# Where the norm work of a fused attention and mixer kernel stands between the exponentials

## The chip, the cores and the metric

The kernel runs on one core of a Trainium2 chip. The metric is the device time of one execution in microseconds (us), the median of five runs. The engines are named as the profile names them: PE (TensorE; PEld is its weight load), DVE (VectorE), ACT (ScalarE), POOL (GpSimd) and SP (SyncE, which here only issues transfers).

## The reference

The input is q, k and v of 8 batches, 12 heads, 448 positions and 64 features, in float32. For each head, rows of q and k are divided by their norm, and attention with temperature tau = 0.1 is taken over them. The heads are then joined to x of 448 x 768 per batch, and a mixer follows.

```
q_n = q / (norm(q) + 1e-6);  k_n = k / (norm(k) + 1e-6)
attn = softmax(q_n @ k_n.T / 0.1);  x = attn @ v         # heads joined to [8, 448, 768]
h = relu(x.T @ w_tok1) @ w_tok2;    u = x + h.T          # w_tok1 448x256, w_tok2 256x448
out = u + relu(u @ w_ch1) @ w_ch2                        # w_ch1 768x1536, w_ch2 1536x768
```

## The kernel before, in words

**Pairs and slots.** The work is cut into 48 pairs of heads, six for a batch. The main loop has one slot for each pair, `i`. In slot i the scores of pair i are made, the product with v of pair i-1 is taken, and the two token matmuls follow for an earlier pair. After the six pairs of a batch its channel mixer (`m_ch1`, `m_ch2`) stands in a queue, from which `feed` takes pieces and puts them between the attention steps of later slots. Everything is in one written order (`tc.manual_schedule`): each engine carries out its own instructions in the order of the program text, and semaphores between engines keep the data right.

**One slot on PE and ACT.** `score(i, c)` for c = 0, 1, 2 makes two matmuls into a tile `psS`, of which there are two buffers, and one exp on ACT (line 298, `pt<-psS`). `score_x(i)` makes one more matmul and exp (line 305, `psX`). Because there are two `psS` buffers, the second matmul pair of slot i+1, `score(i+1, 1)`, can start only when the exp of `score(i, 2)` has been taken. ACT also takes the relu of each `m_ch1` piece (line 387, `gt<-psG`). `next_qk(i+1)` transposes the scaled q and k of the next pair on PE into `pst` (line 239 for the 384 main positions, lines 243 and 244 for the 64 others) and DVE copies them out (line 257). `pv` writes `psO`; DVE takes a reciprocal and multiplies (lines 323 and 324). `m_tok1` writes `psR`, which DVE turns to `r` (line 341); `m_tok2` multiplies `r` (line 357, `psU`).

**The norm work.** A pair p is prepared some slots ahead in four steps:

- `norm_begin(p)`: the squares of q and of k (line 174 on ACT, line 176 on DVE or POOL) into a tile `sq` of two buffers. A pair with p % 3 = 0 also squares the 64 rest positions of its half of a batch, three pairs together, into the single tile `sqx`.
- `norm_sums(p)`: DVE sums them over the features (line 189; line 193 for `sqx`).
- `rnorms(n, c0, c1)`: for half n (three pairs, 45 columns) ACT makes ln, exp, ln, exp (lines 197 to 200) on columns c0 to c1, which gives the inverse norms. Columns 0 to 21 hold the rest positions and the first pair, 21 to 45 the two other pairs. This is called a round below, and a round over columns 0 to 21 or 21 to 45 half a round.
- `norm_scale(p)`: POOL multiplies k and q by them into `kq` (line 207; lines 213 and 218 for the rest positions of a half). For pairs below 15 PE transposes `kq`, later ones go by transposing transfers.

Tables give the slot of each step: `early_sq` for the squares, `sum_at` one slot later, `rn_at` for the rounds, `sc_at` for the scaling (two slots before the pair's own slot up to pair 14). In slots 1 to 5 and from 7 on the loop body was, in this order: scores 0 and 1, sums, rounds, squares and scaling (in this or the other order), casts of v, and then the rest of the slot with `score(i, 2)`. Slot 6 (`FIRST`) has a body of its own.

The lines that matter in the old text:

```
early_sq = {3: 0, 4: 1, 5: 1, 6: 3, 7: 4, 8: 5, 9: 6, 10: 7, 11: 7, 12: 8, 13: 9, 14: 9, 15: 10, 16: 11, 17: 11}
sum_at = at({p: s + 1 for p, s in sq_slot.items()})
for c0, c1 in ((0, 21), (21, 45)) if n < 6 else ((0, 45),):
    s = 1 + sq_slot[3 * n + (0 if c1 == 21 else 2)]
```

Of the kernel before, what the change touches and what calls it, by code (L numbers as in the profile page):

```python
# [22 lines left out]
def kernel(  # L23
# [12 lines left out]
    nc = tc.nc  # L36
# [16 lines left out]
    NPAIR = H // 2  # L53
# [16 lines left out]
    ps = ctx.enter_context(tc.tile_pool(name="ps", bufs=4, space=bass.MemoryType.PSUM))  # L70
# [107 lines left out]
    def squares(p, eq, ek):  # L178
        sq[p] = nrm.tile([P, 2, 2 * NC, E], FP32, name=f"sq_{p}", tag="sq")
        for a, (eng, src) in enumerate(((eq, mh(qm, p)), (ek, mh(km, p)))):  # L180
            square(eng, sq[p][:, a], src.rearrange("p g c e -> p (g c) e"))
# [13 lines left out]
    def rnorms(n, c0=0, c1=45):  # L195
        ssq, rn = ssqs[n % 3][:, c0:c1], rns[n % 3][:, c0:c1]
        nc.scalar.activation(out=rn, in_=ssq, func=AF.Ln, bias=tiny[:])
        nc.scalar.activation(out=rn, in_=rn, func=AF.Exp, scale=0.5)
        nc.scalar.activation(out=rn, in_=rn, func=AF.Ln, bias=eps[:])
        nc.scalar.activation(out=rn, in_=rn, func=AF.Exp, scale=-1.0)  # L200
# [90 lines left out]
    def score(p, c, fill=0):  # L291
        qk, pt = qks[p], pts[p % 2]
        psS = ps2.tile([P, 2, 512], FP32, name=f"psS_{p}_{c}", tag="s")
        busy(psS[:, 0, :], fill)
        for g in range(2):
            r = slice(E * g, E * g + E)
            nc.tensor.matmul(psS[:, g, 0:S], qk[r, P * c:P * (c + 1)], qk[r, 512:512 + S], start=True, stop=True)  # L297
        nc.scalar.activation(out=pt[:, 2 * S * c:2 * S * (c + 1)].rearrange("p (g s) -> p g s", g=2),  # L298
                             in_=psS[:, :, 0:S], func=AF.Exp, scale=inv_tau)

    def score_x(p):
        qk, pt = qks[p], pts[p % 2]
        psX = ps.tile([P, 512], FP32, name=f"psX_{p}", tag="b")
        nc.tensor.matmul(psX[:, 0:S], qk[:, P * NC:P * (NC + 1)], qk[:, 512:512 + S], start=True, stop=True)  # L304
        nc.scalar.activation(out=pt[:, PX:PX + S], in_=psX[:, 0:S], func=AF.Exp, scale=inv_tau)  # L305
# [28 lines left out]
    def m_tok1(p):  # L334
        psR = ps.tile([P, TT, P], FP32, name=f"psR_{p}", tag="b")
        for tt in range(TT):
            for m in range(NC + 1):
                nc.tensor.matmul(psR[:, tt, :], w1t[:, m, tt * P:(tt + 1) * P], xs[p][:, m, :],  # L338
                                 start=(m == 0), stop=(m == NC))
        rs[p] = att.tile([P, TT, P], FP16, name=f"r_{p}", tag="r")  # L340
        nc.vector.tensor_scalar_max(out=rs[p][:], in0=psR[:], scalar1=0.0)  # L341
# [83 lines left out]
    def feed(budget, least=0.0):  # L425
        fed[0] += budget
        done = 0.0
        while queue and (fed[0] > queue[0][0] / 2 or done < least):
            t, fn = queue.pop(0)
            fn()  # L430
            fed[0] -= t
            done += t

    def at(slots):
        got = {}
        for p, s in slots.items():
            got.setdefault(s, []).append(p)
        return got


    FIRST = NPAIR
    early_sq = {3: 0, 4: 1, 5: 1, 6: 3, 7: 4, 8: 5, 9: 6, 10: 7, 11: 7, 12: 8, 13: 9, 14: 9, 15: 10, 16: 11, 17: 11}
    sq_slot = {p: early_sq.get(p, p - 6) for p in range(3, NP_ALL)}
    sq_at = at(sq_slot)
    sum_at = at({p: s + 1 for p, s in sq_slot.items()})

    rn_at = {}
    for n in range(1, NHALF):
        for c0, c1 in ((0, 21), (21, 45)) if n < 6 else ((0, 45),):
            s = 1 + sq_slot[3 * n + (0 if c1 == 21 else 2)]  # L450
            rn_at.setdefault(s, []).append((n, c0, c1))
    sc_at = at({p: {7: 6}.get(p, p - 2 if p < DMA_FROM else p - 3) for p in range(3, NP_ALL)})
# [14 lines left out]
    def norm_begin(p, eq, ek):  # L467
        squares(p, eq, ek)
        if p % HP == 0:
            squares_x(p // HP, eq, ek)  # L470

    def norm_sums(p):
        sums(p)
        if p % HP == 0:
            sums_x(p // HP)
# [6 lines left out]
    with tc.manual_schedule():  # L482
# [77 lines left out]
        for i in range(NP_ALL + 2):  # L560
            for n in qk_at.get(i, ()):
                load_q(n)
                load_k(n)
            for b in x_at.get(i, ()):
                load_xq(b)
                load_xk(b)
            for n in v_at.get(i, ()):
                load_v(n)
            for b in xv_at.get(i, ()):
                load_xv(b)  # L570
            if DMA_FROM <= i + 2 < NP_ALL:
                dma_tpose(i + 2)
            if i - 2 in X_DMA:
                x_tpose(i - 2)
            for p in ut_at.get(i, ()):
                u_tpose(p)

            left = next((t + 1 - i for t in sorted(tok2_at) if t >= i + (i == FIRST) and
                         any(p % NPAIR == NPAIR - 1 for p in tok2_at[t])), 6)
            if FIRST <= i < 2 * NPAIR:  # L580
                quota = max(len(queue) - 6, 0) * ns(S, DT) / (2 * NPAIR - i)
            else:
                quota = max(sum(t for t, _ in queue) - 2000.0, 0.0) / left
            def next_qk(p):
                if p < min(DMA_FROM, NP_ALL):
                    qk_copy(p, tpose(p))

            def tok2(p):
                m_tok2(p)
                if p % NPAIR == NPAIR - 1:  # L590
                    queue.extend(ch_units(p // NPAIR))

            def norm_rn():
                for n, c0, c1 in rn_at.get(i, ()):
                    rnorms(n, c0, c1)

            if i == FIRST:
                m_tok1(i - 2)
                pv(i - 1, 0)
                pv(i - 1, 1)  # L600
                tok2(i - 2)
                m_tok1(i - 1)
                next_qk(i)
                tok2(i - 1)
                for p in sum_at[i]:
                    norm_sums(p)
                feed(0.0, 1000.0)
                score(i, 0)
                norm_rn()
                score(i, 1)  # L610
                feed(0.0, 1000.0)
            elif 0 < i < NP_ALL:
                score(i, 0, 2 if i < 4 else 0)
                score(i, 1)
            if i != FIRST:
                for p in sum_at.get(i, ()):
                    norm_sums(p)
                norm_rn()

            if i >= FIRST:  # L620
                for p in sc_at.get(i, ()):
                    norm_scale(p, nc.gpsimd)
            for p in sq_at.get(i, ()):
                norm_begin(p, nc.scalar if p < 18 else nc.gpsimd, nc.scalar if p == 3 else nc.vector if 9 <= p < 12 else nc.gpsimd)
            if i < FIRST:
                for p in sc_at.get(i, ()):
                    norm_scale(p, nc.gpsimd)
            for n in cast_at.get(i, ()):
                cast_v(n)
            if i in (2, 5):  # L630
                weights_ch1(i // 4)
            if i in (7, 8):
                weights_ch2(i - 7)

            if i < FIRST:
                if i:
                    pv(i - 1, 0)
                if i:
                    score(i, 2)
                    score_x(i)  # L640
                if i + 1 < FIRST:
                    next_qk(i + 1)
                for p in tok_at.get(i, ()):
                    m_tok1(p)
                if i:
                    pv(i - 1, 1)
                for p in tok2_at.get(i, ()):
                    tok2(p)
            elif i == FIRST:
                score(i, 2)  # L650
                score_x(i)
                feed(0.0, 1000.0)
                next_qk(i + 1)
                feed(0.0, 1000.0)
            else:
                feed(quota * 0.25)
                next_qk(i + 1)
                if i <= NP_ALL:
                    pv(i - 1, 0)
                for p in tok_at.get(i, ()):  # L660
                    m_tok1(p)
                feed(quota * 0.25, 400.0)
                if i < NP_ALL:
                    score(i, 2)
                    score_x(i)
                for p in tok2_at.get(i, ()):
                    tok2(p)
                feed(quota * 0.25)
                if i <= NP_ALL:
                    pv(i - 1, 1)  # L670
                feed(quota * 0.25)
            if i == 2:
                place_w2()
# [38 lines left out]
```

## Time and profile before

| what | value |
|---|---|
| median of 5 runs | 408.36 us (408.28 to 410.18) |
| the profiled execution | 409.4 us, its span 407.3 us |
| granted PE clock, mean | 0.985 |
| PE busy | 390.9 us, 96% of the span |
| ACT, POOL, DVE busy | 228.5 us, 208.2 us, 203.2 us |
| slots on PE | slot 6 from about 40, slot 7 from 51.03, 8 from 54.95, 9 from 62.12, 10 from 67.45, 11 from 72.85, 12 from 81.44 us |

In the profile's timeline a row gives the start in us, the length, the engine, the line, the output and input tiles, the shape and a count (`x2` is two instructions merged in one row). Square brackets at its end give the idle time of the engine ahead of the row, and which instruction ended it. The start of a slot is read as the start of its first two `psS` matmuls. PE matmuls overlap in the records, so a wait is better measured between the starts of rows than by the bracket.

### The profile page before, as it was taken

Reading aid. Unit: us, or ns where it says so; the run is one execution under the profiler, and the core shown is the slowest. Engines: PE = TensorE matmul, PEld = TensorE weight load, DVE = VectorE, ACT = ScalarE, POOL = GpSimd, SP = SyncE. Lnnn points to the kernel's source line nnn. Section 1 sums busy time; section 2 is a strip of 40 time slices with the busy share of each in tenths; the row PEclk is TensorE's granted clock in tenths of the full one; section 3 lists DMA queues with packets and bytes.
Section 4 is the critical chain, followed back from the end, with each engine's and each line's share of the span. In section 5 each row is a group of like instructions: output and inputs, shape, how many; then the busy total and the mean of one; then the engine's idle time right before and its main releaser. Section 6 shows DMA issues by size and latency. Waiting matters only on the chain.

```text
span 407.3 us, 9113 instructions
## 1 busy us (share of the span) xinstructions
PE 390.9 (96%) x3646; PEld 226.4 (56%) x3646; DVE 203.2 (50%) x461; ACT 228.5 (56%) x415; POOL 208.2 (51%) x308
## 2 busy tenths in 40 slices
PE   7699989999999999999999999999999999999995
PEld 2366446565555564565555565565555565565562
DVE  5688668565445555436453655446444343232021
ACT  5898599863566547574566445664756435611400
POOL 4877369992093858567592928567673500000000
PEclk9689999999999999999999999999999999999999
DMA  8999999979893798979896698969882643013012
GB/s 218 260 229 258 254 228 207 247 146 226 161 256 76 228 168 214 183 154 203 174 269 101 194 167 202 221 141 236 183 144 50 138 99 66 15 54 103 2 77 77
DMA packets 137194, 67.51 MB, mean 166 GB/s; under 512 B 93184, under 2 KB 133568, under 8 KB 137152
## 3 DMA queue, kind: packets, MB, share of 16 engines
q1 hardware_dynamic: 132976, 61.36, 70.0%
q0 software_dynamic: 3632, 5.18, 7.1%
q8 instruction: 28, 0.46, 0.5%
q10 hardware_dynamic: 544, 0.39, 0.3%
q14 instruction: 14, 0.11, 0.1%
HBM read 43.38 MB, written 11.01 MB: 134 GB/s over the span
## 4 chain that ended last, share of the span: by engine, by line
PE 75%; POOL 7%; ACT 6%; issue 4%; DVE 4%; DMA 3%; SPq 1%; ACTq 0%; POOLq 0%; DVEq 0%
PE psF L399 24%; PE psG L385 23%; PE psO L318 7%; PE psS L297 7%; PE psR L338 4%; PE psU L357 4%; ACT pt L298 3%; PE psX L304 3%; DMA xq<-in_q_dram 2%; POOL kq L207 2%; PE psO L320 2%; POOL sq L176 2%; POOL kq L218 1%; DMA km<-in_k_dram 1%; POOL sqx L176 1%
## 5 line engine op out<-in xcount | busy, mean ns | idle before, releaser
L298 ACT ACTIVATE pt<-psS 128x896 f16<-128x896 f32 x141 | 123.9, 915 | 72.1 <-PE psS L297 71.9
L385 PE MATMUL psG<-ut,wc1t 128*128 128x448 f16 x576 | 122.5, 353 | 0.0
L399 PE MATMUL psF<-wc2t,gt 128*128 128x384 f16 x672 | 117.1, 326 | 0.6 <-ACT pt L305 0.6
L387 ACT ACTIVATE gt<-psG 128x448 f16<-128x448 f32 x96 | 52.1, 544 | 78.5 <-PE psG L385 78.3
L207 POOL TENSOR_TENSOR kq<-km,rn 128x384 f16<-128x384 f32 x47 | 39.0, 829 | 105.1 <-ACT rn L200 100.9
L399 PEld LDWEIGHTS <-gt 128*128 128x128 f16 x672 | 63.4, 98 | 42.6 <-issue 4.7
L385 PEld LDWEIGHTS <-wc1t 128*128 128x128 f16 x576 | 52.5, 98 | 46.0 <-issue 5.4
L402 DVE TENSOR_TENSOR ost<-psF,ur 128x384 f32<-128x384 f32 x56 | 31.2, 557 | 82.0 <-PE psF L399 79.1
L318 PEld LDWEIGHTS <-pt 128*128 128x128 f16 x1152 | 52.6, 98 | 16.6 <-issue 5.7
L318 PE MATMUL psO<-vt,pt 128*128 128x65 f16 x1152 | 58.2, 195 | 0.0
L189 DVE TENSOR_REDUCE ssq<-sq 128x12 f32<-128x768 f32 (+1 forms) x49 | 45.2, 931 | 17.2 <-POOL sq L176 14.4
L297 PE MATMUL psS<-qk 64*128 64x448 f16 x282 | 44.3, 361 | 3.1 <-ACT pt L298 3.1
L324 DVE TENSOR_TENSOR x<-psO,rec 128x256 f16<-128x256 f32 x96 | 40.8, 425 | 3.3
L320 PE MATMUL psO<-vx,pt 128*128 128x130 f16 x192 | 42.1, 219 | 0.0
L207 POOL TENSOR_TENSOR kq<-qm,rn 128x384 f16<-128x384 f32 x47 | 38.8, 826 | 0.0
L323 DVE RECIPROCAL rec<-psO 128x4 f32<-128x4 f32 x96 | 17.1, 178 | 42.4 <-PE psO L320 42.1
L176 POOL TENSOR_TENSOR sq<-km 128x384 f32<-128x384 f32 x43 | 35.3, 822 | 2.9 <-DMA km<-in_k_dram 2.7
L367 DVE TENSOR_TENSOR ut<-psU,xT 128x448 f16<-128x448 f32 (+2 forms) x39 | 17.6, 477 | 25.3 <-PE psU L357 18.5
L338 PE MATMUL psR<-x,w1t 128*128 128x128 f16 x384 | 29.4, 219 | 0.1
L297 PEld LDWEIGHTS <-qk 64*128 64x128 f16 x282 | 10.8, 94 | 33.1 <-issue 28.8
L357 PE MATMUL psU<-w2t,r 128*128 128x448 f16 x96 | 25.9, 353 | 1.7 <-DVE r L341 0.7
L305 ACT ACTIVATE pt<-psX 128x448 f16<-128x448 f32 x48 | 26.1, 544 | 0.0
(75 smaller groups left out, 340.4 us busy)
## 6 DMA issues: line engine op xcount, KB each, us to landing
vm<-in_v_dram SPq DMA_DIRECT2D x16, 576.0 KB, 6.7
out_dram<-ost SPq DMA_DIRECT2D x24, 384.0 KB, 2.9
qm<-in_q_dram SPq DMA_DIRECT2D x15, 576.0 KB, 4.9
km<-in_k_dram SPq DMA_DIRECT2D x15, 576.0 KB, 6.8
wc1t<-in_moe_w_ch_dram POOLq DMA_DIRECT2D x2, 1152.0 KB, 13.5
wc2t<-in_moe_w_ch_dram POOLq DMA_DIRECT2D x2, 1152.0 KB, 12.7
out_dram<-ost SPq DMA_DIRECT2D x8, 192.0 KB, 2.8
xq<-in_q_dram SPq DMA_DIRECT2D x7, 192.0 KB, 8.9
```

The lines of the kernel that those rows point to most:

```text
L176: eng.tensor_tensor(out=out, in0=src, in1=src, op=ALU.mult)
L189: nc.vector.tensor_reduce(out=ssqs[p // HP % 3][:, lo + 6 * a0:lo + 6 * a1], in_=sq[p][:, a0:a1].rearrange("p a g e -> p (a g) e"), axis=A ...
L207: eng.tensor_tensor(out=kqs[n % 2][:, j, a, 0:NC, :].rearrange("p c (g e) -> p g c e", g=2), in0=src, in1=_bcast_free(rn, E), op=ALU.mult)
L297: nc.tensor.matmul(psS[:, g, 0:S], qk[r, P * c:P * (c + 1)], qk[r, 512:512 + S], start=True, stop=True)
L298: nc.scalar.activation(out=pt[:, 2 * S * c:2 * S * (c + 1)].rearrange("p (g s) -> p g s", g=2), in_=psS[:, :, 0:S], func=AF.Exp, scale=inv ...
L318: nc.tensor.matmul(psO[:, mm, E1 * g:E1 * (g + 1)], pt[:, at:at + P], vt[:, 2 * j + g, c, 0:E1], start=(g == 0 and c == 0), stop=False)
L320: nc.tensor.matmul(psO[:, mm, :], pt[:, PX + lo:PX + lo + P], vx[:, j, 0:2 * E1], start=False, stop=True)
L338: nc.tensor.matmul(psR[:, tt, :], w1t[:, m, tt * P:(tt + 1) * P], xs[p][:, m, :], start=(m == 0), stop=(m == NC))
L357: nc.tensor.matmul(psU[:], rs[p][:, tt, :], w2t[:, tt, lo:lo + S], start=(tt == 0), stop=by_dma and tt == TT - 1)
L385: nc.tensor.matmul(psG[:], wc1t[:, dt, ct * P:(ct + 1) * P], ut[:, dt, sp], start=(dt == 0), stop=(dt == DT - 1))
L387: nc.scalar.activation(out=gt[:, ct, sp], in_=psG[:], func=AF.Relu)
L399: nc.tensor.matmul(psF[:], gt[:, ct, lo:lo + P], wc2t[:, ct, dh * DH:(dh + 1) * DH], start=(ct == 0), stop=(ct == CT - 1))
```

## The change

The norm work of pairs 9 to 17 is written at other places, and the rounds of halves 4 and 5 are joined.

- Pair 9: its squares stand at the head of slot 6 (they were in the middle of it), q on ACT and k on POOL (k was on DVE). Its sums follow the second score of slot 6, and its half round, `rnorms(3, 0, 21)`, follows in slot 6 after the third `feed`. It was in slot 7.
- Pair 10: squares at the end of slot 6 (were in slot 7), sums behind them.
- Pairs 11 to 17: squares in the slot that they were in (pair 11 in slot 7, 12 in 8, 13 and 14 in 9, 15 in 10, 16 and 17 in 11), but behind the last exp of the slot instead of behind the rounds; sums at the end of that slot instead of in the next one.
- The half round `rnorms(3, 21, 45)` stays in slot 8. Halves 4 and 5 get one round of 45 columns, in slots 10 and 12, for two half rounds each, in slots 9 and 10 and in 11 and 12.
- The squares of k of pairs 12 and 15, and of their rest positions, go from POOL to DVE. Those of pairs 10 and 11 stay on DVE.

The order of instructions on PE and on SP is the same in both kernels. ACT has eight instructions less, DVE two more and POOL two less. Waits on semaphores differ where the order behind them does.

```diff
-    early_sq = {... 8: 5, 9: 6, 10: 7, 11: 7, 12: 8, ...}
+    early_sq = {... 8: 5, 9: 5, 10: 6, 11: 7, 12: 8, ...}
...
-    sum_at = at({p: s + 1 for p, s in sq_slot.items()})
+    sum_at = at({p: s + 1 for p, s in sq_slot.items() if p < 8 or p >= 18})
...
-        for c0, c1 in ((0, 21), (21, 45)) if n < 6 else ((0, 45),):
+        for c0, c1 in ((0, 21), (21, 45)) if n < 4 else ((0, 45),):
...
+            def next_sq(ps):
+                for p in ps:
+                    norm_begin(p, nc.scalar if p < 18 else nc.gpsimd, nc.scalar if p == 3 else nc.vector if p in (10, 11, 12, 15) else nc.gpsimd)
+
             if i == FIRST:
+                next_sq([9])
                 m_tok1(i - 2)
...
-                for p in sum_at[i]:
-                    norm_sums(p)
+                norm_sums(8)
                 feed(0.0, 1000.0)
                 score(i, 0)
-                norm_rn()
+                rnorms(2, 21, 45)
                 score(i, 1)
+                norm_sums(9)
                 feed(0.0, 1000.0)
...
-            for p in sq_at.get(i, ()):
-                norm_begin(p, nc.scalar if p < 18 else nc.gpsimd, nc.scalar if p == 3 else nc.vector if 9 <= p < 12 else nc.gpsimd)
+            if i < FIRST or i >= 2 * NPAIR:
+                next_sq([p for p in sq_at.get(i, ()) if p != 9])
...
                 score(i, 2)
                 score_x(i)
                 feed(0.0, 1000.0)
+                rnorms(3, 0, 21)
                 next_qk(i + 1)
+                next_sq(sq_at[i])
+                norm_sums(10)
                 feed(0.0, 1000.0)
...
                     score(i, 2)
                     score_x(i)
+                if i < 2 * NPAIR:
+                    next_sq(sq_at[i])
                 for p in tok2_at.get(i, ()):
                     tok2(p)
                 feed(quota * 0.25)
                 if i <= NP_ALL:
                     pv(i - 1, 1)
+                if i < 2 * NPAIR:
+                    for p in sq_at[i]:
+                        norm_sums(p)
                 feed(quota * 0.25)
```

## The prediction

> **What bounds the kernel now.** I read the page first: its busy times name PE.
>
> ```profile
> PE 390.9 (96%) x3646; PEld 226.4 (56%) x3646; DVE 203.2 (50%) x461; ACT 228.5 (56%) x415; POOL 208.2 (51%) x308
> ```
>
> PE has no slack over the span, so a change of norm work can only take away time in which PE stands. The change lies between 40 and 82 us; there I read the PE timeline, and for each bracket in it the timeline of the engine that it names.
>
> ```profile
> 51.03 0.55 PE L297 MATMUL psS<-qk 64*128 64x448 f16 x4
> ...
> 54.95 0.36 PE L297 MATMUL psS<-qk 64*128 64x448 f16 x2
> 56.46 0.37 PE L297 MATMUL psS<-qk 64*128 64x448 f16 x2 [1.14 <-ACT pt L298]
> 56.76 0.51 PE L239 MATMUL pst<-id,kq 128*128 128x128 f16 x6
> 57.99 0.23 PE L243 MATMUL pst<-id,kq 128*128 128x128 f16 x1 [0.72 <-POOL kq L218]
> ...
> 66.28 0.55 PE L357 MATMUL psU<-w2t,r 128*128 128x448 f16 x2 [0.21 <-DVE r L341]
> ...
> 68.09 0.37 PE L297 MATMUL psS<-qk 64*128 64x448 f16 x2 [0.28 <-ACT pt L298]
> ```
>
> Slot 7 shows a free start: four psS matmuls in 0.55, so the second two begin 0.19 behind the first. From starts: slot 8's second pair came at 56.46 instead of 55.14, a loss of 1.32; its line 243 at 57.99 instead of 57.10 (0.34 behind line 239, as elsewhere), 0.89; slot 9's psU at 66.28 instead of 65.91, 0.37; slot 10's second pair at 68.09 instead of 67.64, 0.45; slot 11's four took 0.79, 0.24. Together 3.27 us. Cross-check: slots 8, 9 and 10 last 7.17, 5.33 and 5.40, and less these losses 4.96, 4.96 and 4.95, for equal work. From 82 to 407 us the waits list gives PE three waits, together 1.7 us.
>
> ```profile
> 53.18 0.32 ACT L197 ACTIVATE rn<-ssq,tiny 128x21 f32<-128x21 f32 x1
> ...
> 54.26 0.92 ACT L174 ACTIVATE sq<-qm 128x384 f32<-128x384 f32 x2
> 55.08 0.52 ACT L387 ACTIVATE gt<-psG 128x448 f16<-128x448 f32 x1
> 55.51 0.91 ACT L298 ACTIVATE pt<-psS 128x896 f16<-128x896 f32 x1
> ```
>
> This is slot 7 on ACT. A half round takes 1.08 (53.18 to 54.26), two squares 0.82, and only then comes the exp that frees the psS buffer for 56.46. With three exps at 0.81, the exp of psX 0.43 and one relu 0.43, ACT needs 5.19 us in such a slot, more than PE's 4.95. The half round of half 3 ends at 54.35, so POOL's scaling of pair 9 runs 54.48 to 57.93: the second wait.
>
> **The change, part by part.** I lay the new order out with the same step lengths. Start to start on ACT: exp 0.81, psX 0.43, relu 0.43, square 0.41, round 1.08. On DVE: sums 0.86, rest sums 0.66, copy of pst 0.58, reciprocal and multiply 0.55. On POOL: 0.79, four steps of a pair with rest positions 3.45.
>
> Slot 6: pair 9's squares cost nothing. ACT stands from 40.0 to 45.15 and POOL from 40.4 to 47.66; q and k of half 3, issued at 26.87 and 27.46, landed 6.2 and 7.4 us later. Without that cover the squares would hold ACT for 0.8. Sums of pair 9 end on DVE at 46.9. ACT then runs exp 48.69, psX, relu, half round 50.35 to 51.43, square of pair 10, relu, and slot 7's exps from 52.27, 0.7 later than before; slot 7's third scores (53.87) need the first of them, done at 53.2.
>
> Slot 7: the relu ends at 54.38 and `score(7, 2)`'s exp at 55.20, because no half round stands before it. Slot 8's second pair starts at 55.27: 1.32 becomes 0.13, a gain of 1.19. POOL scales pair 9 from 51.65 to 55.10, and line 243 would come at 55.91: 0.89 goes. Running gain 2.08; slot 9 would start at 60.05.
>
> Slot 8: exps from 56.04, half round 57.66 to 58.75, relu, third exp 59.2, psX, squares 60.43 to 61.25. POOL scales pair 10 from 58.97 to 60.6, and PE reaches its q part at 60.71. DVE squares k of pair 12 from 58.57, and then waits for ACT: sums from 61.0. Its chain (sums, rest sums, copy, reciprocal, multiply, r) puts r at 63.7 and psU at 64.1, where PE would be at 63.8. So the wait at psU stays at about 0.3; only its cause is new.
>
> Slots 9 to 11: slot 9 has no round, so the third exp ends in time and 0.45 goes; slot 11 loses its half round and 0.24 goes. Pairs 13 and 14 add two sums at the end of slot 9, ahead of the copy of pair 11; DVE follows psU's late start, so slot 10's r comes about 0.2 after PE wants it. That is given back.
>
> Slot 10: the joined round waits for pair 14's sums (about 67.7 to 68.0). Behind it in ACT's queue stand a relu, the third exp and psX, which PE wants only 2.6 later; behind its result stands POOL's scaling of pair 12, 3.45 long, ending at 72.5, where PE wants the last part at about 72.5. Before, this scaling had 4 us of slack (done at 71.04, used at 75.05). So the cover is gone.
>
> Without contention the sum is 2.08 + 0.45 + 0.24 less about 0.3 given back: 2.5 us.
>
> **DVE against POOL.** The squares of k of pairs 10, 11, 12 and 15 are now DVE instructions with two SBUF inputs beside a busy POOL. In the old stretch DVE's three such squares ran at 0.55 while POOL stood still. One place in the trace has both busy:
>
> ```profile
> 10.78 0.82 POOL L176 TENSOR_TENSOR sq<-km 128x384 f32<-128x384 f32 x1
> 11.56 0.66 POOL L213 TENSOR_TENSOR kq<-xq,rn 64x256 f16<-64x256 f32 x1
> ```
>
> ```profile
> 10.86 0.89 DVE L213 TENSOR_TENSOR kq<-xq,rn 64x128 f16<-64x128 f32 x1 [0.67 <-ACT rn L200]
> ```
>
> DVE's 0.89 compares with about 0.29 by the line through its free rows (0.55 at 384 elements, 0.35 at 192): it stood until POOL's instruction ended at 11.60. POOL's next lost some 0.05 (0.66 against 0.61 by its own line), so a 384 element square may cost POOL about 0.3. The bounds for a square are 0 and a whole POOL instruction, 0.82. I take the row. Pairs 10 and 11 have room. Pair 12: POOL's q part ends at 60.85 instead of 60.6, so PE waits 0.2. Pair 15: POOL's scaling of pair 12 ends some 0.45 later, and PE waits 0.5 to 0.6. Together about 0.7, which leaves 1.8 us.
>
> [...]
>
> From slot 12 on: pair 15's scaling waits for the joined round of slot 12 and ends near 86 us instead of 82.4, but SP issues its transposing transfer only at 92.96 (about 91 now), so 5 us of cover remain. POOL then stood from 94.3 to 111.57, which takes up the delay. The weight transfers on POOL's queue (59.77 and 63.55) are issued some 3 us earlier. SP's order is the same; its q load for half 6 waits for pair 11's scaling, which comes earlier. Everything later follows PE, so the gain stays.
>
> The profiled execution took 409.4 with a span of 407.3, 1.0 above the median; I subtract the difference from the median: 408.36 - 1.8 = 406.6. Its span should fall to about 405.5.
>
> **The rivals.** *No contention worth counting*: 2.5 us, and 3.1 if the r chain also keeps up: 405.2 to 405.9. For it: the squares may fall between POOL's instructions. Against it: the row at 10.86.
>
> [...]
>
> *The joined round holds the queue* (slower). If pair 14's sums come late, ACT stands at line 197 with exps behind it, and POOL's scaling of pair 12 and PE's transposes follow one for one. Sums at 70 instead of 68 take the gain away; at 71.3 or later it is slower by over 0.3%. What could do it is POOL, which must issue a transfer (0.88), scale pair 11 (1.6) and square two k (1.6) between 60.6 and 66. By these rows it is done at 64.7, which speaks against it. Price at 3.5 us lateness: 408.36 - 1.8 + 3.5 = about 410.
>
> **How the numbers follow.** Forecast 0.5, no contention 0.2, the stall moves 0.2, the queue 0.1. About 0.3%, 1.23 us, is what a measurement of this kernel can tell from no change; faster means below 407.13. The forecast's own range, from the bounds of contention, is 406.0 to 407.2. Faster gets all of the second case and nearly all of the first, with a little of the third: 0.72. Same 0.18, slower 0.1. The range 405.2 to 407.8 takes in the second case and most of the third.
>
> **What would show it.** Right: slot 8's two psS pairs within 0.35 of each other; line 243 of slot 8 without a bracket; slots 9 to 11 free of ACT's brackets; POOL's scaling of pair 9 ending near 55; a wait of about 0.5 on POOL at slot 11's line 243, and DVE's squares of pairs 12 and 15 above 0.55. Wrong: an exp bracket still above 0.5 in slots 8 to 11, ACT idle in front of line 197 for over 1 us in slot 10, or new PE waits behind 82 us.

## The result and the profile after

The changed kernel takes 406.86 us (27 runs, 405.75 to 409.39) where the kernel before, run on the same chip, takes 408.80 us: a ratio of 0.9954, 95% interval 0.9943 to 0.9965. A second set of runs gave 0.9954 again (0.9920 to 0.9987). The profiled execution has a span of 404.8 us, against 407.3.

The page's first lines, of the changed kernel:

```profile
PE 389.4 (96%) x3646; PEld 225.7 (56%) x3646; DVE 205.2 (51%) x463; ACT 226.5 (56%) x407; POOL 208.9 (52%) x306
```

PE bounds it as before. Its timeline, at the places that the prediction named:

```profile
53.96 0.79 PE L297 MATMUL psS<-qk 64*128 64x448 f16 x4
54.68 0.51 PE L239 MATMUL pst<-id,kq 128*128 128x128 f16 x6
55.02 0.22 PE L243 MATMUL pst<-id,kq 128*128 128x128 f16 x1
...
63.09 0.55 PE L357 MATMUL psU<-w2t,r 128*128 128x448 f16 x2
64.26 0.55 PE L297 MATMUL psS<-qk 64*128 64x448 f16 x4
...
71.07 0.50 PE L239 MATMUL pst<-id,kq 128*128 128x128 f16 x6
72.17 0.23 PE L243 MATMUL pst<-id,kq 128*128 128x128 f16 x1 [0.60 <-POOL kq L218]
```

Slot 8's four psS matmuls are now one row of 0.79, where 0.55 is free: 0.24 is left of 1.32, so the second pair stands about 0.43 behind the first, a little above the 0.35 that the prediction gave as a sign. Its line 243 follows line 239 by 0.34, so 0.89 went whole. Slot 9's psU is 0.08 late, slot 10's four psS are free. What is new is the last row: 1.10 behind line 239 instead of 0.34, a wait of 0.76 on POOL.

The waits of PE, first from 40 to 82 us, then from 80 us to the end, of each list the line that counts (engine, tile and line that waited, who released it, us in total, times, longest):

```profile
PE pst L243 <- POOL kq L218: 0.6, 1, 0.6
...
```

```profile
...
PE psG L385 <- DVE ut L367: 0.3, 1, 0.3
```

This one is new behind 82 us; it stands at 262.43 us, in slot 35. (The three other rows of that list, 1.9 us together, are those of the kernel before, where they made 1.7; one of them now counts two waits instead of one.) ACT's timeline shows the joined round of slot 10 behind an exp and with no bracket: the round found pair 14's sums ready, though only just: DVE's row of sums ends at 66.77, and the round starts at 66.81.

```profile
65.11 1.74 ACT L298 ACTIVATE pt<-psS 128x896 f16<-128x896 f32 x2
66.81 0.34 ACT L197 ACTIVATE rn<-ssq,tiny 128x45 f32<-128x45 f32 x1
```

Below, "the stretch" is the time from slot 6's psX (line 304) to slot 12's psX. Nearly all of the change lies in it. It was 40.72 in the profile before and is 38.84 now: 1.88 less. A stand is time in which PE waits.

### The profile page after: what moved, and what is told of

Its sections match the earlier page's. It is cut to its first block, busy times and chain, and to the rows that moved or that the text cites. A ratio compares the mean times of both kernels' runs of the same rounds, so it can differ in the third digit from the quotient of the medians.

```text
span 404.8 us, 9103 instructions
## 1 busy us (share of the span) xinstructions
PE 389.4 (96%) x3646; PEld 225.7 (56%) x3646; DVE 205.2 (51%) x463; ACT 226.5 (56%) x407; POOL 208.9 (52%) x306
## 4 chain that ended last, share of the span: by engine, by line
PE 78%; ACT 7%; DVE 4%; POOL 4%; issue 3%; DMA 2%; SPq 1%; POOLq 0%; DVEq 0%
PE psF L399 26%; PE psG L385 23%; PE psO L318 7%; PE psS L297 7%; PE psR L338 4%; PE psU L357 4%; ACT pt L298 3%; PE psX L304 3%; PE psO L320 2%; POOL sq L176 1%; DMA qm<-in_q_dram 1%; POOL sqx L176 1%; POOL kq L207 1%; DVE x L324 1%; PE pst L239 1%
```

## The experiments

All runs together; "clock at 0.50" is how long the granted clock stood at 0.50, in the start-up and in slots 6 to 12 (a slice of 2 us with a mean clock of c holds 4 x (1 - c) us of it, since windows of 0.25 us show 0.50 or 1.00 and another mean only where the clock changes). Ratios are against the kernel before on the same chip.

| kernel | median us | ratio, interval | stretch | slot 35 | clock at 0.50 |
|---|---|---|---|---|---|
| before, profile shown above | 408.36 | | 40.72 | 7.52 | 10.24 / 0 |
| before, second profile (e8) | 409.27, one run | | 42.00 | 7.53 | 6.84 / 3.40 |
| before, third profile (e11) | 409.39, one run | | 41.95 | 7.53 | 6.84 / 3.40 |
| changed | 406.86 | 0.9954, 0.9943 to 0.9965 | 38.84 | 7.89 | 6.80 / 0 |
| changed again (e9) | 406.81 | 0.9954, 0.9920 to 0.9987 | 38.82 | 8.05 | 6.80 / 0 |
| e1 pair 9 alone | 406.06 | 0.9931, 0.9910 to 0.9952 | 38.94 | 8.08 | 3.44 / 0 |
| e2 pair 9 back | 412.30 | 1.0068, 1.0048 to 1.0089 | 43.22 | 8.84 | 3.40 / 3.44 |
| e3 rounds split | 406.11 | 0.9927, 0.9906 to 0.9948 | 38.32 | 7.52 | 6.84 / 0 |
| e10 rounds split, again | 406.72 | 0.9941, 0.9917 to 0.9964 | 38.28 | 8.15 | 3.44 / 0 |
| e4 half 4 split | 406.18 | 0.9934, 0.9903 to 0.9965 | 38.28 | 8.32 | 3.40 / 0 |
| e5 k of 15 on ACT | 407.45 | 0.9955, 0.9937 to 0.9972 | 38.33 | 8.72 | 6.84 / 0 |
| e7 e4 and e5 together | 405.92 | 0.9915, 0.9883 to 0.9947 | 38.38 | 8.12 | 3.40 / 0 |
| e6 round late | 409.70 | 0.9998, 0.9975 to 1.0021 | 40.82 | 8.19 | 6.84 / 0 |
| e12 k on POOL | 411.45 | 1.0080, 1.0052 to 1.0107 | 44.26 | 7.55 | 3.44 / 3.40 |

**e1: pair 9's early norm work alone, in the kernel before.**

```diff
             if i == FIRST:
+                norm_begin(9, nc.scalar, nc.gpsimd)
                 m_tok1(i - 2)
...
                 score(i, 1)
+                norm_sums(9)
                 feed(0.0, 1000.0)
...
                 feed(0.0, 1000.0)
+                rnorms(3, 0, 21)
                 next_qk(i + 1)
```

(and pair 9 left out of `sq_at`, `sum_at` and `rn_at` at its old places)

> The kernel before, with pair 9 alone moved: its squares to the head of slot 6 (k on POOL), its sums behind the second score and its half round behind the third feed of slot 6. All else is as before. I measure the stretch on PE from slot 6's psX matmul to slot 12's: 40.72 us before, 38.84 in the changed kernel, which keeps the start of the execution out. Theory (slot 8's two waits were the half round of half 3; the other parts of the change only trade waits): slot 8 loses 0.3 to 0.5 instead of 2.2, and ACT, which still needs 5.19 us in slots 8 to 10, gives 0.2 to 0.5 of it back: stretch 39.0 to 39.4, time ratio near 0.996. Rival (the squares behind the last exp and the fewer rounds make the gain): under 0.9 gained, stretch 39.8 or more.

The stretch was 38.94: 1.78 of the change's 1.88, a little better than the lower end of the theory's numbers. PE's timeline in slot 8:

```profile
54.88 0.36 PE L297 MATMUL psS<-qk 64*128 64x448 f16 x2 [0.39 <-ACT pt L298]
55.18 0.51 PE L239 MATMUL pst<-id,kq 128*128 128x128 f16 x6
55.52 0.22 PE L243 MATMUL pst<-id,kq 128*128 128x128 f16 x1
```

One of the two stands of slot 8 is gone, and the other is 0.56 (54.88 instead of 54.32, which is 0.19 behind the first pair). The rest of the change takes away about as much in slots 8 to 11 as it adds at line 243 of slot 11, where e1 has no wait.

**e2: the change without pair 9's early work.**

```diff
-                next_sq([9])
...
-                norm_sums(9)
...
-                rnorms(3, 0, 21)
...
+            if i == FIRST:
+                norm_begin(9, nc.scalar, nc.vector)
+            if i == FIRST + 1:
+                norm_sums(9)
+                rnorms(3, 0, 21)
```

> The changed kernel, with pair 9 put back: squares in the middle of slot 6 (k on DVE), sums and half round in slot 7. All other parts of the change stay. Theory: POOL's scaling of pair 9 runs late again and slot 8's line 243 stands 1.5 to 2 us; slot 8 as a whole loses 2.2 to 2.6; the other parts are worth nothing by themselves, since the waits that they remove in slots 9 to 11 (1.06 in sum) are as long as those that they bring (1.15). Stretch from slot 6's psX to slot 12's 40.7 to 41.2, time as before. Rival (fewer rounds on ACT count for themselves): 0.7 or more of the gain stays, stretch 40.0 or less.

The stretch was 43.22, 2.0 beyond the theory's upper end. Pair 10's sums now stand in DVE's queue ahead of pair 9's, so the half round waits for them. ACT and PE in slots 7 and 8:

```profile
53.49 0.31 ACT L197 ACTIVATE rn<-ssq,tiny 128x21 f32<-128x21 f32 x1 [0.51 <-DVE ssq L193]
```

```profile
55.95 0.36 PE L297 MATMUL psS<-qk 64*128 64x448 f16 x2 [0.94 <-ACT pt L298]
58.40 0.29 PE L243 MATMUL pst<-id,kq 128*128 128x128 f16 x1 [1.49 <-POOL kq L218]
```

The second stand is twice that of the kernel before. And from 58.08 on the granted clock was 0.50: rows that take 0.61 (psR x8) and 1.30 (psG x6) took 1.06 and 1.81. That second part no theory had. The run is therefore no clean measure of what pair 9 is worth, and e1 is.

**e3 and e10: the rounds of halves 4 and 5 as half rounds, all else changed.** The second run stands beside the changed kernel's second.

```diff
-        for c0, c1 in ((0, 21), (21, 45)) if n < 4 else ((0, 45),):
+        for c0, c1 in ((0, 21), (21, 45)) if n < 6 else ((0, 45),):
```

> The changed kernel, with the rounds of halves 4 and 5 as two half rounds each again (slots 9 and 10, 11 and 12); squares and sums stay where the change put them. Theory (the joined round of half 4 makes POOL's scaling of pair 12 late, and ACT has room for the extra half round in slot 9, where it idles 0.68 us): the wait of 0.76 at slot 11's line 243 goes and nothing takes its place: stretch from slot 6's psX to slot 12's 38.1 to 38.3, ratio to before 0.993 to 0.995. Rival (fewer rounds are what saved ACT): waits of exps come back in slots 10 and 11, stretch 39.2 or more.

> The changed kernel with the rounds of halves 4 and 5 as half rounds, a second time, beside the changed kernel itself. Theory: the stretch repeats at 38.32 within 0.1 and the time is 0.5 us below that of the changed kernel of the same call, if slot 35 averages out. Rival: slot 35 repeats at 7.52 and belongs to the kernel, and then the split gains 0.9.

The stretch was 38.32 and 38.28: the join costs 0.52. It is the difference of two terms, and "nothing takes its place" was wrong: the 0.76 at line 243 goes, but slot 10's psU comes 0.45 late instead of 0.22. In time, e3 by itself looked 0.75 us better than the changed kernel, but beside it the two took 406.72 and 406.81, so the half microsecond is seen in the stretch and not in the time. Slot 35 was 7.52 and 8.15, so its length belongs neither to this kernel nor to the theory's average.

**e4: half 4 alone split** (`n < 5` in the same line).

> The changed kernel with only half 4's round split again into its two half rounds; half 5 keeps its joined round in slot 12. Theory (the join costs only where its scaling has no cover, that is pair 12's in slot 11): the same as with both rounds split, 38.1 to 38.35 us from slot 6's psX to slot 12's psX against 38.84 of the changed kernel, no wait above 0.3 at line 243 of slot 11, and no new PE wait behind slot 12. Rival (ACT's eight instructions less per half round matter by themselves): 38.5 or more, since half 5's join alone would then give less than both splits.

38.28, as with both split, and no wait on line 243. Half 5's join costs PE nothing; half 4's is the one without cover, as the prediction had it. A wait of 0.28 on `r` (0.45 from starts) is left at slot 10's psU. ACT makes a half round in slot 9 again, so its squares of pairs 13 and 14 start 18.45 behind slot 6's psX instead of 18.21, and DVE's sums and `r` come later with them.

**e5: the squares of k of pair 15 on ACT.**

```diff
-nc.scalar if p == 3 else nc.vector if p in (10, 11, 12, 15) else nc.gpsimd)
+nc.scalar if p in (3, 15) else nc.vector if p in (10, 11, 12) else nc.gpsimd)
```

> The changed kernel, with the squares of k of pair 15 and of its rest positions on ACT instead of DVE. DVE then has no instruction with two SBUF inputs beside POOL's scaling of pair 12. Theory (the shared read of DVE and POOL adds 0.53 us to that scaling): it takes 3.45 us instead of 3.98, and the wait at slot 11's line 243 falls from 0.76 to 0.2 or 0.3: stretch from slot 6's psX to slot 12's 38.3 to 38.4. Rival (the joined round alone makes it late): the wait stays at 0.7 and the stretch at 38.8.

38.33. POOL's timeline in slot 10, first of the changed kernel, then of e5:

```profile
68.13 1.24 POOL L207 TENSOR_TENSOR kq<-km,rn 128x384 f16<-128x384 f32 x1 [4.27 <-ACT rn L200]
69.33 0.94 POOL L207 TENSOR_TENSOR kq<-qm,rn 128x384 f16<-128x384 f32 x1
```

```profile
68.29 0.83 POOL L207 TENSOR_TENSOR kq<-km,rn 128x384 f16<-128x384 f32 x1 [4.27 <-ACT rn L200]
69.09 0.83 POOL L207 TENSOR_TENSOR kq<-qm,rn 128x384 f16<-128x384 f32 x1
```

Without DVE's squares beside it, POOL's two steps take 0.83 each instead of 1.24 and 0.94. The loss of 0.52 is the contention, shown by taking it away. In the time it is not seen: the median is 407.45, and slot 35 took 8.72 here.

**e7: e4 and e5 together.**

> The changed kernel with half 4's round split and the squares of k of pair 15 on ACT, the two removals that each gave 0.51 to 0.52 us in the stretch alone. Theory (both act on the same wait, line 243 of slot 11, which was 0.76 in all, so they don't add up): 38.05 to 38.25 us from slot 6's psX to slot 12's psX. Rival (they add up): 37.8 or less. Total time 405.5 to 407.0, unless slot 35 gives back differently.

38.38, no less than either alone, so the two don't add up: they act on the one wait, which each split alone already ends. The theory's own lower figure (38.05 to 38.25) was missed by 0.13. The time was the lowest median of all, 405.92, but its interval overlaps that of the changed kernel; that it is faster than the changed kernel is not shown.

**e6: half 4's joined round later, behind psX of slot 10.**

```diff
-            if i != FIRST:
+            if i not in (FIRST, 10):
                 norm_rn()
...
+                if i == 10:
+                    norm_rn()
+                    norm_scale(12, nc.gpsimd)
+                    cast_v(4)
```

> The changed kernel with half 4's joined round put behind the exp of psX in slot 10 (and pair 12's scaling and the cast of v behind it), so that it begins about 2.8 us later without holding any exp. It tests the price that the prediction gave lateness of this round: each microsecond of lateness behind it follows one for one to line 243 of slot 11. Theory: round begins about 69.6 instead of 66.8, the wait at line 243 grows from 0.76 by 2.2 to 2.8, and the stretch from slot 6's psX to slot 12's psX becomes 41.0 to 41.6; a kernel of about the time before. Rival (the delay is hidden in part, since pair 12's scaling then runs beside no square of DVE, and PE has other work to do): less than 40.3. A third possibility, from what was seen when pair 9 was put back: after the stand the granted PE clock falls for some 4 us, which adds over a microsecond, 42 or more.

The stretch was 40.82, 1.98 more, between the theory and its rival. Measured from slot 6's psX the round starts 2.50 later, not 2.8 (23.23 behind it instead of 20.73). POOL's scaling takes 3.45 instead of 3.98, as no square of DVE runs beside it. 2.50 - 0.53 = 1.97: with both numbers as they came, lateness follows one for one to line 243.

```profile
75.13 0.23 PE L243 MATMUL pst<-id,kq 128*128 128x128 f16 x1 [1.49 <-POOL kq L218]
```

The prediction's rival *The joined round holds the queue* had its mechanism right, then; only its condition, sums that come late, did not occur. The clock didn't fall (1.00 in both steps from 73.56 to 80.38).

**e12: the squares of k of pairs 12 and 15 back on POOL.**

```diff
-nc.scalar if p == 3 else nc.vector if p in (10, 11, 12, 15) else nc.gpsimd)
+nc.scalar if p == 3 else nc.vector if p in (10, 11) else nc.gpsimd)
```

> The changed kernel with the squares of k of pairs 12 and 15, and of their rest positions, back on POOL, as in the kernel before; all else of the change stays. It asks whether the move to DVE, which the prediction charged 0.7 us for contention and the changed kernel shows as a wait of 0.76 at line 243 of slot 11, was worth its price. Theory (the move is needed by the sums at the end of the slot): in slot 8 POOL reaches pair 12's square only behind pair 10's scaling and a transfer that it issues, about 60.65, so DVE's sums (59.98 in the changed kernel) start about 61.5 and r and psU come 1.5 later; in slot 10 POOL reaches pair 15's squares only behind the casts of v, one of which waits for its load until 75.8, so the sums stand on DVE from 71 to 77 with the copy of pst, x and r behind them, and PE's psU of slot 11 comes about 4.3 later. The wait of 0.5 at line 243 goes. Stretch from slot 6's psX to slot 12's psX: 38.84 - 0.5 + 1.5 + 4.3 = about 44, and 1 to 1.6 more if the granted clock falls behind the stands; a kernel slower than before, about 412. Rival (only the contention counts): 38.3, and a time 0.5 below the changed kernel.

44.26, near the expected 44, but by other terms. DVE's timeline in slot 10, then PE's:

```profile
74.87 0.96 DVE L189 TENSOR_REDUCE ssq<-sq 128x12 f32<-128x768 f32 x1 [4.19 <-POOL sq L176]
```

```profile
77.10 0.35 PE L304 MATMUL psX<-qk 128*128 128x448 f16 x1 [2.18 <-DVE qk L257]
77.98 0.55 PE L357 MATMUL psU<-w2t,r 128*128 128x448 f16 x2 [0.54 <-DVE r L341]
```

The wait at line 243 falls from 0.76 to 0.22 from starts, as with e5. But DVE stood 4.19 for POOL's square with the copy of pst behind it, and PE lost 2.9 there from starts (2.24 at psX, 0.68 at psU), not 4.3: the cast that waited for its load until 75.83 in the changed kernel had no such wait here. In slot 9 PE lost 1.05 more at psU and 0.40 at psX, together about the 1.5 expected. Then the clock stood at 0.50 from 78.64 to 82.05, which made up the rest, some 1.6. So the move to DVE costs 0.5 in contention, and without it the stretch is 5.4 longer (44.26 instead of 38.84), about 3.8 of it from waits: the move is what allows sums at the end of the slot.

**e8, e11, e9: the kernel before and the changed one, unaltered, profiled again.**

> The kernel before, profiled a second time. It tells what of the differences between profiles belongs to the execution and not to the kernel. Theory: the stretch from slot 6's psX to slot 12's psX is again 40.72 within 0.1; slot 0 to slot 1 (5.48 before, 4.38 to 4.78 in all others) varies with the clock granted at 14 to 22 us, so it may be near 4.5 here; slot 35's length (7.52 before) stays within 0.2. Rival: slot 35's length varies from execution to execution of one kernel by 0.5 or more, and then what was handed back there is no property of the change.

> The kernel before, profiled a third time. Slot 7 (psX of 7 to psX of 8), which holds the two stands of 1.32 and 0.89, took 6.59 in the first profile with a granted clock of 1.00 behind them and 8.22 in the second with a clock of 0.50 from about 57 to 60 us. Theory: it is one of these two values within 0.2, by whether the clock falls behind the stands; all else of slots 6 to 12 repeats within 0.4. Rival: another value, and then the clock is not the only thing that varies there.

> The changed kernel, profiled and timed a second time. Theory: slots 6 to 12 belong to the kernel and repeat (psX of slot 6 to psX of slot 12 in 38.84 within 0.1, since no stand of PE is long enough for the clock to fall in it), while the start-up (slot 0 to 1, 4.38 in the first profile) and slot 35 (7.89) belong to the execution and may lie anywhere between 4.2 and 5.7 and between 7.5 and 8.9. Rival: slot 35 repeats at 7.89 within 0.1, and then the hand-back there belongs to the kernel.

The changed kernel's stretch repeats (38.82, with line 243 again held by POOL, 0.59). The kernel before took 42.00 and 41.95 instead of 40.72. The longer part lies behind slot 8's two stands: psX of slot 7 to that of slot 8 took 6.59, 8.22 and 8.06, and 0.35 of that came back at slot 9's psU, which was late in the first profile alone. The stands themselves were alike (brackets 1.15 and 0.72 in both later profiles, 1.14 and 0.72 in the first). What differed is the clock. A stand's length, which e9's theory gives as the condition, does not tell by itself when it falls: no step at 0.50 followed e6's bracket of 1.49, and one followed the brackets of 1.15 and 0.72 here.

**Where the clock falls.** The stretches at 0.50 in the table are 3.40 to 3.44, 6.80 to 6.84 and 10.24 long: one, two or three times 3.41 us. So I laid a grid of 3.41 us steps on from the end of each execution's slow start-up, and read how long PE was busy in each step. Four executions have a step at 0.50 in slots 6 to 12, and each began on a grid line to within 0.05 us. Here are the windows on that grid. The columns are the window, its length, the busy time of PE, PEld, DVE, ACT and POOL with their instructions, the granted clock, the DMA share and GB/s. The kernel before, first profile:

```profile
53.84:57.25 3.41, 2.27 (x28) 1.25 (x27) 2.44 (x5) 3.38 (x8) 2.77 (x4) 1.00 1.25 287
57.25:60.66 3.41, 2.69 (x33) 1.73 (x32) 1.71 (x5) 3.09 (x9) 3.21 (x6) 1.00 1.27 153
```

Its second profile (e8):

```profile
53.61:57.02 3.41, 1.55 (x17) 0.81 (x17) 2.35 (x5) 3.41 (x7) 3.27 (x6) 1.00 1.28 263
57.03:60.44 3.41, 3.41 (x28) 2.26 (x26) 1.66 (x4) 1.84 (x7) 3.28 (x6) 0.50 0.83 140
```

Its third (e11):

```profile
54.37:57.78 3.41, 1.88 (x29) 1.40 (x29) 2.44 (x5) 3.35 (x7) 3.27 (x5) 1.00 1.29 156
57.79:61.20 3.41, 3.41 (x15) 1.29 (x13) 0.93 (x3) 1.89 (x6) 3.28 (x7) 0.50 1.23 260
```

The change without pair 9's early work (e2):

```profile
54.67:58.08 3.41, 1.30 (x11) 0.52 (x10) 1.83 (x4) 3.41 (x6) 3.21 (x5) 1.00 1.83 241
58.08:61.49 3.41, 3.09 (x27) 2.37 (x28) 2.03 (x5) 1.25 (x5) 3.21 (x6) 0.50 0.60 154
```

Squares of k on POOL (e12):

```profile
75.23:78.64 3.41, 1.01 (x8) 0.48 (x8) 2.66 (x6) 1.94 (x4) 3.41 (x6) 1.00 1.18 296
78.64:82.05 3.41, 3.41 (x25) 1.86 (x22) 0.80 (x2) 0.76 (x2) 1.38 (x2) 0.50 1.23 244
```

The round late (e6):

```profile
73.56:76.97 3.41, 1.92 (x30) 1.46 (x29) 1.46 (x5) 0.85 (x2) 3.21 (x6) 1.00 1.29 196
76.97:80.38 3.41, 3.41 (x34) 1.93 (x33) 0.76 (x2) 2.67 (x6) 3.33 (x6) 1.00 1.10 255
```

In each pair the second row's clock follows the first row's busy time. After 1.01, 1.30, 1.55 and 1.88 us of PE work the clock was 0.50 for one step; after 1.92 and 2.27 it stayed at 1.00. From the end of the start-up to about 120 us no step of the 14 profiled executions breaks this order. Outside that part some do: in the start-up of e3, e5 and e6 the clock fell behind a step with about 2.0 us of PE work (1.96 to 2.02, summed from windows of 0.25 us), and near the end of e6 it stayed at 1.00 behind a step with 1.80 (from 401.23; the mean clock on record, 0.992, leaves room for the start-up's 6.84 us at 0.50 alone). So the summed length of PE's rows, whose ends are modelled, tells nearly but not exactly when the clock falls, and no sharp bound is shown. In the first profile of the kernel before a grid line at 57.25 falls between the two stands, and the two steps hold 2.27 and 2.69 us of work. In the two others one step holds both stands. So the same stands cost 2.2 us, or 2.2 and a further 1.2 to 1.3 in the stretch, by where the grid lies in the execution. The changed kernel never came below 2.8 us of work in a step there.

## Why the prediction was right, and where it was not

**The sum held.** It said 1.8 us less in slots 8 to 11; measured against the same profile, 1.88. What was to be left: 0.13 at slot 8's second pair, 0.2 at pair 10's q part, about 0.3 and 0.2 at the two psU, 0.5 to 0.6 at line 243 of slot 11. Measured from starts: 0.24, 0.09, 0.08, 0.22 and 0.76, together 1.39, and 3.27 - 1.39 = 1.88. Each stand came where it was named, but the sizes miss by up to 0.2 both ways, so that the sum is closer than its terms is partly luck. (The prediction also takes off "about 0.3" as given back where its text names 0.2 for slot 10's r.) POOL's scaling of pair 9 ends at 54.73, where near 55 was written, and that match is luck: slot 7 started 1.00 earlier than in the profile before, so the scaling ends 4.70 behind slot 7's first psS matmul where the prediction's 55.10 means 4.07. It was in time for line 243 by 0.3.

**Slot 8's stands and their cause.** e1 shows that pair 9's half round out of the way of `score(7, 2)`'s exp, and its scaling early, give nearly the whole. The other parts (squares behind the last exp, sums early, joined rounds, k on DVE) exchange one wait for another: 0.1 net.

**The joined round.** That pair 12's scaling loses its cover was right; e4 and e6 show it, with the price of one for one. Without contention it would be 0.23 late (e5: line 243 0.57 behind line 239 instead of 0.34), and contention adds 0.53.

**Contention: the size right, the side wrong.** The prediction let DVE stand and charged POOL 0.3 for a square; POOL's first step lost 0.41 and its second 0.11. The sign "DVE's squares of pairs 12 and 15 above 0.55" is wrong for the 384 element squares. DVE's timeline in slots 6 and 10:

```profile
49.47 0.80 DVE L176 TENSOR_TENSOR sq<-km 128x384 f32<-128x384 f32 x1
...
68.13 0.55 DVE L176 TENSOR_TENSOR sq<-km 128x384 f32<-128x384 f32 x1
68.59 0.99 DVE L176 TENSOR_TENSOR sqx<-xk 128x192 f32<-128x192 f32 x1
```

At 68.13 both engines start in the same instant, and it is POOL that takes 1.24 instead of 0.83 while DVE runs free. DVE's next square, of rest positions, starts at 68.59 with POOL's first step at work until 69.37, and its 0.35 becomes 0.99. At 49.47 POOL had begun first (49.02), and DVE takes 0.80. In these rows either of the two can be the one that takes longer. Why they do is not shown: that it is a shared read, as e5's theory has it, was the author's estimate, and e5 shows that POOL's 0.52 go with DVE's squares. The prediction's row at 10.86 does not show a stand to the end of POOL's instruction either: DVE ends at 11.75, 0.15 behind it, and its own work there is 0.29 by the prediction's line.

**"Everything later follows PE, so the gain stays": wrong by 0.4 to 0.5.** Slot 35 took 7.52 to 7.53 in all three profiles of the kernel before, and 7.89 and 8.05 in the changed one. PE waits there for DVE's `ut`, and that for a transposing transfer of x (line 331), which landed 0.10 before `ut` starts. SP issued it 1.86 us earlier than before (257.91 instead of 259.77) while PE was 2.85 earlier. The transfers ahead of it on SP's queue, loads and a transposing one that holds SP for 3.25 us (3.40 before), did not move as far. The other kernels gave back from 0 to 1.3 us there, and two profiles of one kernel 0 and 0.6. What sets the pace of that queue stays open. This hand-back is a term that the prediction put at nothing.

**What one profile could not tell.** The profile before happened to be one in which the clock held in slot 8 and the start-up was slow for three steps of 3.41 us instead of two; its span (407.3) is that of the other two (407.2 and 407.3). Against those two, the stretch is 3.1 us shorter, the start-up (slot 0's psX to slot 6's) about equal (32.08 and 31.62 before, 31.88 and 31.75 after), and 0.3 to 0.5 is given back behind slot 12. Against the first profile the span is 2.5 shorter: 1.88 in the stretch and 0.98 in the start-up, less 0.3 given back.

The medians differ by 1.9 to 2.5. Part of that goes with the clock. The mean granted clock is on record for runs without a profile too, and one step at 0.50 takes some 0.004 from it (3.41 x 0.5 of a span of 407 us). The three profiles of the kernel before have 0.985 and 0.986. Here are the 65 runs of the kernel before that were made beside the experiments, and the 36 of the changed one; they come from several chips, so this is a rough split (in e9's set, on one chip, 8 of 13 and 0 of 9 are at 0.987 or less):

| kernel | runs at 0.987 or less, median us | runs above, median us |
|---|---|---|
| before | 28, 409.59 | 37, 408.41 |
| changed | 3, 408.61 | 33, 406.75 |

Runs with a lower mean clock are longer and are rarer after the change. Among the runs above 0.987 the kernels are 1.66 apart, among all 2.3 (409.17 and 406.84). So it is partly luck that the time fell by 1.94 where 1.8 was forecast (406.86 against 406.6): the forecast left out both the 0.4 to 0.5 that slot 35 gives back and the clock, and the two have opposite signs. Where the steps at 0.50 lay in runs without a profile, in the start-up or in slot 8, is not on record.

The rival *No contention* is refuted by e5's 0.51, *The stall moves*, which has 0.2 in the chances, by the sum of 1.88, and *The joined round holds the queue* by the missing bracket at line 197. No run shows a square that costs POOL a whole instruction of 0.82, the upper bound in the forecast; POOL's two steps lost 0.41 and 0.11.

## What to carry to other kernels

Look first for the few instructions that stand between an exp and the matmul that needs it; here one pair's half round, moved ahead of it, brought 1.78 of 1.88 us. Before joining two small rounds, ask what stands behind the later one: work that had 4 us of slack became the last to arrive, and its lateness went through (e6: the last part 1.97 us later, the stretch 1.98 longer). Price a stand of PE not by its length alone but together with its neighbours: here two stands with brackets of 1.15 and 0.72 inside one step of 3.41 us cost the clock as well (e8, e11), a further 1.2 to 1.3 us.

## What the runs showed of the hardware

Four times in slots 6 to 12 (e2, e8, e11 and e12) the clock fell to 0.50 for one step of 3.41 us, each time after a step in which PE's rows sum to 1.01 to 1.88 us. PE never stood idle for a whole step: the longest bracket in any of the four is 2.18 us (e12), and in the kernel before 1.15 (e8, e11). The step with 1.88 us of PE work in it is e11's. Where the bound lies is not shown: the clock stayed at 1.00 behind 1.92 us in slot 11 of e6 and behind 1.80 near its end, and it fell behind about 2.0 in three start-ups.
